# A written order of TensorE from the 21st attention tile on, and norm bounds of f64 weights from products of bf16 halves

## The chip, the cores and the metric

The kernel runs on one core of a Trainium2 chip. The metric is the device time of one execution in microseconds (us), the median of several runs. A core has five engines that run their own queues of instructions in order: PE (TensorE: matmuls, with their weight loads PEld), DVE (VectorE), ACT (ScalarE), POOL (GpSimd) and SP (SyncE, which here only issues DMAs). They wait for each other by semaphores. TensorE multiplies 128x128 weights (lhsT) with a moving operand (rhs) and adds into PSUM, which has eight banks per partition; the other engines work on SBUF and PSUM.

## The reference

Three blocks follow each other: attention with a threshold instead of a full softmax, a gated MLP with RMS norm whose weights come as f64, and a mixture of 8 experts whose gates are balanced by eight rounds of row and column normalisation.

```python
# q, k, v: 4 batches x 8 heads x 576 x 64
scores = scale * np.matmul(q, k.transpose(0, 1, 3, 2))
scores = np.where(scores >= np.max(scores, axis=-1, keepdims=True) - tau, scores, -1e9)
attn = np.exp(scores - np.max(scores, axis=-1, keepdims=True)); attn /= sum + 1e-9
x = attn @ v                                   # as 2304 x 512
xn = x / rms(x) * rms_g
x = silu(xn @ w_gate) * (xn @ w_val) @ w_out   # 512 -> 1536 -> 512, w_* in f64
P = balanced(exp(x @ w_gate2))                 # 2304 x 8
out = sum over e of P[:, e:e+1] * (relu(x @ w1[e]) @ w2[e])   # 512 -> 1024 -> 512
```

## The kernel before

**Precision.** Every f32 operand is written as a sum of two f16 words, high and low, after a scale by a power of two, and a product is three matmuls: high by high, high by low, low by high (`passes`). The scale of a weight comes from a bound on the norms of its columns.

**Attention.** The 36 rows of 128 or 64 queries (4 batches, 4 rows of 128 and one of 64) give 144 attention tiles: a tile is a row and a head (or two heads of the short row). `att_tile` makes S with four matmuls of 128x288 (L303), its row maximum on VectorE (L317), exp on ScalarE (L321), the threshold mask on VectorE (L323), and the two f16 words hl of e on ScalarE (L328) and GpSimd (L329, L330). `turn` transposes hl into eT by a DMA that SP issues. Four tiles later (LAG) `att_values` multiplies eT with v, 14 matmuls or 28 in the short rows (pv, L360). S has two PSUM tiles, pv one. When the 8 tiles of a row are done, `end_main` or `end_rem` divides by the sums and `finish_x` norms the row and transposes it into xnT.

**MLP.** Two rows together are a group j of 256 tokens. `mlp_in(j)` makes for each of 12 blocks f of the hidden width one PSUM tile gv (two halves, gate and value, 12 matmuls of 128x256 each, L557), from which ScalarE's tanh and two VectorE instructions make u (L565 to L567) and ScalarE and GpSimd the two words tT (L571, L572). `mlp_out(j)` makes two PSUM tiles x2 of 36 matmuls of 128x512 (L591), scales them and sends them to memory, transposed later as xo. gv and x2 share two PSUM tiles, tag mm. Groups 0 to 6 run during attention, 7 and 8 behind it.

**The weights of the MLP.** They come as f64. `words` loads a block of 128x512 of them as pairs of 32-bit words; `to_f32` rebuilds f32 from them: a Prelu on ScalarE that rescales the high word (L462), a shift of the low word on VectorE (L463), and an or of both on VectorE (L465). `prep_in` does so for a third of w_gate or w_val (four blocks kk). To bound the norms, ScalarE squares each block in bf16 (L483), and a matmul of 128x512 with the squared g of the RMS norm (gsq, L484) sums the squares of each column over partitions and blocks; VectorE takes the maximum over the 512 columns (L486), and all partitions hold it, since the weight operand is broadcast. Then come the scale, and the two f16 words (L492, L493). `prep_out` does the same for w_out, with squares and their row sums on ScalarE (L517, a Square whose accumulator is read) and a maximum over all partitions by `all_max`: a matmul with the identity and a reduction over 128 columns (L134, L136). `stage` is memory of wo in which three thirds of weights can be converted at a time; psx is one PSUM tile (tag mx) for all of these sums.

**What orders the work.** The code is handed to a scheduler that gives each engine its queue by priorities: attention stands ahead of the MLP (`attention_order`), and within that the scheduler takes what it holds to be ready; so gv, S and pv come in an order that the code doesn't spell out. `issue_after` only ties pv of an old tile behind S of a new one. `prepare` loads and converts q, k and v of the next batch in between. Behind attention a written order of TensorE already exists for the experts. There the weights of the first expert are loaded into w1r and w2r as soon as the memory of attention is free (L785), their maxima taken on VectorE (L790), and w1mxp is the matmul of that maximum.

## Time and profile before

| | us |
|---|---|
| median of 3 runs | 2075.53 (2074.88 to 2076.74) |
| profiled execution | 2072.64 |
| its span | 2070.8 |
| busy: PE | 1937.3 |
| busy: DVE | 1622.1 |
| busy: POOL | 1351.4 |
| busy: ACT | 1297.6 |

The span goes from the first to the last instruction of the profiled execution; the time of that execution is 1.84 us longer. Busy times are shares of the whole span, over stages that differ: the front with the weights' conversion up to about 143 us, attention with the MLP up to 601.6 us, the last groups of the MLP up to 728 us, and the experts. A time within the span is counted from its start.

### The profile page before, as it was taken

How to read it: one execution, taken by the hardware profiler on the slowest of the kernel's cores; microseconds unless marked ns; L12 is line 12 of the kernel's file. 1: busy time of each engine (PE TensorE's matmuls, PEld its weight loads, DVE VectorE, ACT ScalarE, POOL GpSimd, SP SyncE). 2: the span in 40 equal slices, each digit the busy share in tenths (PEclk: the TensorE clock that was granted, in tenths of full speed). 3: DMA queues.
4: the chain of work that ended last, by engine and by line, in shares of the span. 5: the costliest groups of instructions: out<-in, count | busy, mean ns of one | idle time of the engine just before them, and what ended most of it. 6: DMA issues, size and time to landing. Idle time of an engine off the chain costs nothing.

```text
span 2070.8 us, 43792 instructions
## 1 busy us (share of the span) xinstructions
PE 1937.3 (94%) x16462; PEld 1445.0 (70%) x16462; DVE 1622.1 (78%) x3364; ACT 1297.6 (63%) x2804; POOL 1351.4 (65%) x1412
## 2 busy tenths in 40 slices
PE   1558899899999998999999999999999999999998
PEld 0246676777777766777777777777777777777777
DVE  6998777778754546998888888888887888888865
ACT  6998778878753365657555555555555555555542
POOL 0457664666654476777677777776777777777754
PEclk9569999999999999999999999999999999999999
DMA  9987878977748665334434433444443434334332
GB/s 296 261 177 128 163 160 147 184 129 139 129 83 213 144 158 169 110 118 143 128 120 134 131 116 119 130 131 127 128 139 122 122 117 143 120 120 128 105 97 82
DMA packets 373093, 290.46 MB, mean 140 GB/s; under 512 B 286160, under 2 KB 299344, under 8 KB 372880
## 3 DMA queue, kind: packets, MB, share of 16 engines
q1 hardware_dynamic: 371712, 285.81, 53.6%
q8 instruction: 129, 2.11, 0.4%
q0 software_dynamic: 640, 1.84, 0.3%
q14 instruction: 84, 0.69, 0.1%
q10 hardware_dynamic: 528, 0.02, 0.0%
HBM read 195.71 MB, written 21.23 MB: 105 GB/s over the span
## 4 chain that ended last, share of the span: by engine, by line
PE 65%; DVE 3%; POOL 1%; DMA 1%; issue 1%; ACT 1%; SPq 0%; DVEq 0%; POOLq 0%; ACTq 0%
PE P L1127 30%; PE X L1059 17%; PE Z L1059 13%; PE gv L557 3%; PE x L591 2%; DVE w L766 1%; DMA xo<-x2d 1%; DVE acc L1141 0%; SPq L871 0%; DVE h L1038 0%; PE logits L913 0%; DVE lg L1005 0%; POOL w2s L833 0%; DVE w1m L790 0%; POOL h L1038 0%
## 5 line engine op out<-in xcount | busy, mean ns | idle before, releaser
L1127 PE MATMUL P<-w,h 128*128 128x256 f16 x6048 | 769.9, 273 | 2.7 <-DVE acc L1141 1.8
L1127 PEld LDWEIGHTS <-h 128*128 128x128 f16 x6048 | 591.4, 98 | 145.7 <-issue 9.8
L1059 PEld LDWEIGHTS <-w 128*128 128x128 f16 x4032 | 394.6, 98 | 195.6 <-issue 4.6
L1137 DVE SCALAR_TENSOR_TENSOR acc<-P,coef,acc 128x256 f32<-128x256 f32 x882 | 409.7, 477 | 81.7 <-PE P L1127 73.0
L1059 PE MATMUL X<-xo,w 128*128 128x384 f16 x2304 | 437.7, 327 | 1.3 <-ACT u2b L1079 0.9
L1059 PE MATMUL Z<-xo,w 128*128 128x384 f16 x1728 | 327.7, 326 | 1.5 <-DMA xo<-x2d 1.5
L329 POOL TENSOR_TENSOR hl<-e,hl 128x512 f16<-128x512 f32 x144 | 172.9, 1201 | 193.7 <-ACT hl L328 135.6
L557 PE MATMUL gv<-xnT,wg 128*128 128x256 f16 x1296 | 162.9, 274 | 14.7 <-DVE u L567 13.4
L557 PE MATMUL gv<-xnT,wv 128*128 128x256 f16 x1296 | 165.0, 273 | 0.0
L557 PEld LDWEIGHTS <-wg 128*128 128x128 f16 x1296 | 124.7, 98 | 33.7 <-issue 16.0
L591 PE MATMUL x<-wo,tT 128*128 128x512 f16 x648 | 144.2, 379 | 0.0
L323 DVE SCALAR_TENSOR_TENSOR e<-S,nt,e 128x576 f32<-128x576 f32 x144 | 116.5, 811 | 28.5 <-ACT e L321 28.0
L557 PEld LDWEIGHTS <-wv 128*128 128x128 f16 x1296 | 125.5, 98 | 14.7
L317 DVE TENSOR_REDUCE nt<-S 128x1 f32<-128x576 f32 x144 | 106.7, 750 | 25.1 <-PE S L303 22.8
L360 PE MATMUL pv<-vs,eT 128*128 128x64 f16 (+1 forms) x2240 | 97.1, 200 | 30.9 <-DMA eT<-hl 30.8
L360 PEld LDWEIGHTS <-eT 128*128 128x128 f16 (+1 forms) x2240 | 87.3, 105 | 52.9 <-DMA eT<-hl 40.3
L572 POOL TENSOR_TENSOR tT<-u,tT 128x256 f16<-128x256 f32 x108 | 74.9, 695 | 69.7 <-ACT tT L571 69.6
L321 ACT ACTIVATE e<-S,nt,c 128x576 f32<-128x576 f32 x144 | 117.4, 818 | 0.0
L591 PEld LDWEIGHTS <-tT 128*128 128x128 f16 x648 | 62.1, 98 | 70.7
L328 ACT ACTIVATE hl<-e 128x576 f16<-128x576 f32 x144 | 96.8, 677 | 21.3 <-DMA eT<-hl 10.4
L303 PE MATMUL S<-kT,qT 128*128 128x288 f16 (+1 forms) x320 | 65.2, 310 | 26.3 <-DVE e L323 19.7
L766 DVE SCALAR_TENSOR_TENSOR w<-w1r,w_s,w 128x512 f16<-128x512 f32 x64 | 84.1, 1328 | 7.1 <-ACT w L765 7.0
(2536 smaller groups left out, 3623.2 us busy)
## 6 DMA issues: line engine op xcount, KB each, us to landing
xo<-x2s SPq DMA_DIRECT2D x319, 384.0 KB, 3.1
w1r<-in_moe_w_dram SPq DMA_DIRECT2D x17, 1024.0 KB, 5.0
w2r<-in_moe_w_dram SPq DMA_DIRECT2D x17, 1024.0 KB, 6.1
x2s<-xo SPq DMA_DIRECT2D x17, 384.0 KB, 2.8
wgatew<-in_moe_w_gate_dram SPq DMA_DIRECT2D x12, 512.0 KB, 5.6
wo<-in_moe_w_out_dram SPq DMA_DIRECT2D x12, 512.0 KB, 4.6
wvalw<-in_moe_w_val_dram SPq DMA_DIRECT2D x12, 512.0 KB, 5.1
qX<-qT SPq DMA_DIRECT2D x40, 128.0 KB, 2.7
```

The lines of the kernel that those rows point to most:

```text
L317: V.tensor_reduce(mx, sv, AX.XY, ALU.max)
L321: A.activation(ev, sv, AF.Exp, bias=nt[:, 0:1], scale=st["c2"][:, c : c + 1])
L323: V.scalar_tensor_tensor(ev, sv, nt[:, 1:2], ev, ALU.is_ge, ALU.mult, accum_out=sums[:, slot : slot + 1])
L328: A.activation(hl[:, 0:S], e, AF.Copy)
L329: G.tensor_tensor(hl[:, S + REM :], e[:, 0 : NCH * P], hl[:, 0 : NCH * P], ALU.subtract)
L360: T.matmul(o, lhsT=a, rhs=r, start=n == 0, stop=n == len(mm) - 1)
L557: T.matmul(gv[:, a, :], lhsT=w[:, l, kk, f * P : (f + 1) * P], rhs=xt[:, r * KD + kk, :], start=n == 0, stop=n == 3 * KD - 1,)
L591: T.matmul(ps, lhsT=tT[f][:, l, o : o + P], rhs=wo[:, f, r, :], start=n == 0, stop=n == 3 * KF - 1,)
L766: V.scalar_tensor_tensor(dst[1], src, s, dst[0], ALU.mult, ALU.subtract)
L1059: T.matmul(ps, lhsT=w[:, a, l, kk, f * P : (f + 1) * P], rhs=xb[:, r * 2 + kk, :], start=n == 0 and j in (0, 1, 3), stop=n == 5, skip_grou ...
L1127: T.matmul(ps, lhsT=hs[u, ao, f][:, l, jj * P : (jj + 1) * P], rhs=w2[h][:, bo, r, f, :], start=n == 0 and j in (0, 1, 3), stop=n == 5, sk ...
L1137: main[True] = V.scalar_tensor_tensor(y, ps, coef[h][:, i : i + 1], y, ALU.mult, ALU.add)
```

## The change

Two things change.

First, the norms. The columns' sums of squares are no longer made. For each block `gram` multiplies the upper halves of its f32 words, read as bf16 with a step of two, with themselves, in four products of 128x128; all of a third of the weight add into one PSUM tile of 128x128, whose largest entry bounds the norm. VectorE reduces 128 columns instead of 512, and `all_max` takes the maximum over the partitions. g enters as its own maximum, a scale by a power of two (`gn`, `i_g0`, `ig2`). w_out's bounds come the same way, in three groups of four blocks. In `prep_in` the low word is no longer shifted on VectorE: ScalarE copies the 16-bit half that holds its upper bits, scaled and shifted down, into an integer. In `prep_out` the shift stays on VectorE and the Squares go.

Second, the order. From the end of the second row of queries on, TensorE's queue is the order of the code. The MLP becomes a generator: each attention tile now calls `mlp_step`, which gives one gv tile (24 matmuls) or a third of an x2 tile (12 matmuls). A group's steps start WAIT = 3 tiles behind its second row. `prep_out` stands ahead of group 0, with a priority offset of −300.

```diff
-    waiting, spot = [], [0]
+    waiting, spot, ordered = [], [0], []
     LAG = 4
+    WAIT = 3
...
         if len(waiting) == LAG:
-            with tc.issue_after(last.ins):
+            with ExitStack() as es:
+                if not ordered:
+                    es.enter_context(tc.issue_after(last.ins))
                 att_values(*waiting.pop(0))
...
+    gm = small([P, 1], "gmax")
+    V.tensor_reduce(gm, g_sb, AX.X, ALU.max, apply_absolute_value=True)
+    s_g, i_g0 = pow2_scale(all_max(gm, "gmx0", True), 1, 0, "rms")
+    gn = small([P, KD], "gn")
+    V.tensor_scalar(gn, g_sb, s_g[:, 0:1], None, ALU.mult)
+    ig2 = small([P, 1], "ig2")
+    V.tensor_tensor(ig2, i_g0, i_g0, ALU.mult)
+
+    def gram(ps, raw, first, last):
+
+        w = raw.bitcast(BF16).rearrange("p (n t) -> p n t", t=2)
+        for c in range(DM // P):
+            blk = w[:, c * P : (c + 1) * P, 1]
+            T.matmul(
+                ps, lhsT=blk, rhs=blk, start=first and c == 0, stop=last and c == DM // P - 1
+            )
+
+    def gram_bank(name):
+
+        return psx.tile([P, P], F32, tag="mx", name=name, bufs=1)
...
-    def to_f32(dst, word, name):
+    def to_f32(dst, word, name, engine=None):
...
-        V.tensor_scalar(lw, word[:, :, 0], 29, None, ALU.logical_shift_right)
+        if engine is A:
+            half = word.bitcast(U16).rearrange("p n (w t) -> p (n w) t", t=4)
+            A.activation(lw, half[:, :, 1], AF.Copy, scale=2.0**-13, bias=2.0**-15 - 0.5)
+        else:
+            V.tensor_scalar(lw, word[:, :, 0], 29, None, ALU.logical_shift_right)
         di = dst.bitcast(I32)
         V.scalar_tensor_tensor(di, di, 3, lw, ALU.logical_shift_left, ALU.bitwise_or)
-        return lw
...
-        ps = psx.tile([P, DM], F32, tag="mx", name=f"{name}n{gi}", bufs=1)
+        ps = gram_bank(f"{name}n{gi}")
...
-            to_f32(raw[:, kk], wd, f"{name}l{gi}_{kk}")
-            sq = pw.tile([P, 2 * P], F32, tag="u", name=f"{name}q{gi}_{kk}", bufs=2).bitcast(BF16)
-            A.activation(sq, raw[:, kk], AF.Square)
-            T.matmul(ps, lhsT=gsq[:, kk : kk + 1].to_broadcast([P, P]), rhs=sq, start=kk == 0, stop=kk == KD - 1)
-        n2 = small([P, 1], name + "n2", bufs=2)
+            to_f32(raw[:, kk], wd, f"{name}l{gi}_{kk}", A)
+            gram(ps, raw[:, kk], kk == 0, kk == KD - 1)
+        n2 = small([P, 1], "wn2", bufs=2)
         V.tensor_reduce(n2, ps, AX.X, ALU.max)
-        s, inv = norm_scale(n2, 1, 9, f"{name}{gi}")
-        gs = small([P, KD], f"{name}gs{gi}")
-        V.tensor_scalar(gs, g_sb, s[:, 0:1], None, ALU.mult)
+        s, inv = norm_scale(all_max(n2, "wnx"), 1, 9, f"{name}{gi}")
+        gs = small([P, KD], "wgs", bufs=3)
+        V.tensor_scalar(gs, gn, s[:, 0:1], None, ALU.mult)
...
-        V.tensor_scalar(a, i_g, 1.0 / 32.0, None, ALU.mult)
+        V.tensor_scalar(a, i_g, i_g0[:, 0:1], 1.0 / 32.0, ALU.mult, ALU.mult)
         g32.append(a)
-        V.tensor_tensor(igv[:, gi : gi + 1], i_g, i_v, ALU.mult)
+        V.scalar_tensor_tensor(igv[:, gi : gi + 1], i_g, ig2[:, 0:1], i_v, ALU.mult, ALU.mult)
...
-        om = small([P, KF], "om")
+        om = small([P, NG], "om")
         for f in range(KF):
             wd = words(bits[f * P : (f + 1) * P, :], f"wo{f}", ("x2", "x2t")[f % 2])
-            sq = to_f32(wo32[:, f], wd, f"wol{f}").bitcast(BF16)[:, 0:DM]
-            A.activation(sq, wo32[:, f], AF.Square, accum_out=om[:, f : f + 1])
+            to_f32(wo32[:, f], wd, f"wol{f}")
+            if f % n == 0:
+                ps = gram_bank(f"wog{f}")
+            gram(ps, wo32[:, f], f % n == 0, f % n == n - 1)
+            if f % n == n - 1:
+                V.tensor_reduce(om[:, f // n : f // n + 1], ps, AX.X, ALU.max)
         for _ in range(2):
-            V.tensor_tensor(
-                om.rearrange("p (g f) -> p g f", g=NG),
-                om.rearrange("p (g f) -> p g f", g=NG),
-                igv.to_broadcast([P, NG, n]),
-                ALU.mult,
-            )
+            V.tensor_tensor(om, om, igv, ALU.mult)
...
-    def mlp_in(j, hook=None):
+    def in_steps(j, tT, hook=None):
         xt = xnT.pop(j)
-        tT = []
...
+            yield
+
+    def mlp_in(j, hook=None):
+        tT = []
+        for _ in in_steps(j, tT, hook):
+            pass
...
+    def mlp_steps(j):
+        tT = []
+        yield from in_steps(j, tT)
+        yield from out_steps(j, tT)
+
+    def out_steps(j, tT, pool=None):
...
+                if n % KF == KF - 1 and n < 3 * KF - 1:
+                    yield
...
+            if a == 0:
+                yield
...
-            if o == o0 + 2:
+            if o == o0 + 4:
...
+    steps = []
+
+    def mlp_step(t):
+
+        while steps and steps[0][0] <= t:
+            if next(steps[0][1], 0) is None:
+                return
+            steps.pop(0)
...
+    with ExitStack() as order:
+        for t in range(len(row) + LAG):
...
+                for g in done:
+                    (end_main if g["c"] < NCH else end_rem)(g)
+                mlp_step(t)
...
-            i = g["i"]
...
-                    tc.tile_pool(name="psm", bufs=2, space=PSUM, side="right")
-                )
-                for gi in range(NG):
-                    prep_group(gi)
-                first = tc.cur_priority
-                tT = mlp_in(0)
-                prep_out()
-                mlp_out(0, tT)
-            elif i is not None and i % 2 == 1 and i < len(tiles) - 3:
-                mlp_out(i // 2, mlp_in(i // 2))
+                i = g["i"]
+                if i == 1:
+                    pse_cm.__exit__(None, None, None)
+                    psm = ctx.enter_context(
+                        tc.tile_pool(name="psm", bufs=2, space=PSUM, side="right")
+                    )
+                    for gi in range(NG):
+                        prep_group(gi)
+                    first = tc.cur_priority
+                    with tc.high_priority(offset=-300):
+                        prep_out()
+                    order.enter_context(tc.manual_schedule(engines={mybir.EngineType.PE}))
+                    ordered.append(True)
+                if i is not None and i % 2 == 1 and i < len(tiles) - 3:
+                    steps.append((t + WAIT, mlp_steps(i // 2)))
+        while steps:
+            mlp_step(t + WAIT)
     psa_cm.__exit__(None, None, None)
     pa_cm.__exit__(None, None, None)
```

On TensorE around the first gv tile, before (a name reads tile_batch_row_head for S, tile_group_block for gv, and the first matmul of each run of one tile is shown):

```order
L360 MATMUL pv0_2_1860<-vs0_0_229,eT0_2_3_1875 128x64
...
L557 MATMUL gv0_0_1228<-xnT0_595,wg_102 128x256
...
L557 MATMUL gv0_1_1260<-xnT0_595,wg_102 128x256
...
L303 MATMUL S0_3_0_2013<-kT0_0_171,qT0_3_794 128x288
...
L360 MATMUL pv0_2_1860<-vs0_1_232,eT0_2_4_1915 128x64
...
L303 MATMUL S0_3_1_2048<-kT0_0_171,qT0_3_794 128x288
...
L360 MATMUL pv0_2_1860<-vs0_1_232,eT0_2_5_1950 128x64
...
L557 MATMUL gv0_2_1291<-xnT0_595,wg_102 128x256
```

and in the changed kernel:

```order
L458 MATMUL wog4_1340<-wo_102 128x128
...
L579 MATMUL gv0_0_1585<-xnT0_610,wg_100 128x256
...
L303 MATMUL S0_2_7_1617<-kT0_1_205,qT0_2_526 128x288
...
L362 MATMUL pv0_2_1480<-vs0_0_244,eT0_2_3_1495 128x64
...
L579 MATMUL gv0_1_1651<-xnT0_610,wg_100 128x256
...
L303 MATMUL S0_3_0_1683<-kT0_0_186,qT0_3_809 128x288
...
L362 MATMUL pv0_2_1480<-vs0_1_247,eT0_2_4_1535 128x64
...
L579 MATMUL gv0_2_1718<-xnT0_610,wg_100 128x256
```

Before, gv0_0 and gv0_1 stand together and then two pairs of S and pv; in the changed kernel each gv tile of 24 matmuls is followed by the S and pv of one attention tile. wog4 are the products of w_out's halves.

On TensorE at the end of attention, before (pv3_4 are the last values of batch 3; the last line of them here is the last tile's, 28 matmuls):

```order
L360 MATMUL pv3_4_9764<-vs3_0_8033,eT3_4_0_9662 64x64
...
L557 MATMUL gv6_5_8578<-xnT6_7929,wg_102 128x256
...
L360 MATMUL pv3_4_9764<-vs3_1_8128,eT3_4_6_9793 64x64
...
L557 MATMUL gv6_6_8609<-xnT6_7929,wv_103 128x256
...
L557 MATMUL gv6_11_8765<-xnT6_7929,wg_102 128x256
...
L591 MATMUL x2_12_8796<-wo_104,tT6_0_8450 128x512
...
L591 MATMUL x2_13_8842<-wo_104,tT6_0_8450 128x512
...
L557 MATMUL gv7_0_9932<-xnT7_9189,wg_102 128x256
```

and in the changed kernel:

```order
L628 MATMUL x2_12_9565<-wo_102,tT6_4_9062 128x512
...
L628 MATMUL x2_12_9565<-wo_102,tT6_8_9324 128x512
...
L628 MATMUL x2_13_9716<-wo_102,tT6_0_8791 128x512
...
L303 MATMUL S3_4_6_9777<-kT3_1_7392,qT3_4_9227 64x288
...
L362 MATMUL pv3_4_9871<-vs3_0_7612,eT3_4_0_9703 64x64
...
L579 MATMUL gv7_1_10072<-xnT7_8841,wg_100 128x256
...
L362 MATMUL pv3_4_9871<-vs3_1_7811,eT3_4_6_9900 64x64
...
L579 MATMUL gv7_3_10138<-xnT7_8841,wg_100 128x256
```

What was behind the last pv (gv6_6 to gv6_11, x2_12, x2_13) stands ahead of it now; gv7_0 does too.

On VectorE behind attention, before:

```order
L567 SCALAR_TENSOR_TENSOR u7_0_9957<-u7_0_9957,gv7_0_9932 128x256
L566 SCALAR_TENSOR_TENSOR u7_1_9989<-u7_1_9989,gv7_1_9964 128x256
L567 SCALAR_TENSOR_TENSOR u7_1_9989<-u7_1_9989,gv7_1_9964 128x256
L790 TENSOR_REDUCE w1m_9926<-w1r1_9928 128x1
L566 SCALAR_TENSOR_TENSOR u7_2_10021<-u7_2_10021,gv7_2_9996 128x256
L567 SCALAR_TENSOR_TENSOR u7_2_10021<-u7_2_10021,gv7_2_9996 128x256
L790 TENSOR_REDUCE w1m_9926<-w1r1_9928 128x1
L566 SCALAR_TENSOR_TENSOR u7_3_10055<-u7_3_10055,gv7_3_10030 128x256
L567 SCALAR_TENSOR_TENSOR u7_3_10055<-u7_3_10055,gv7_3_10030 128x256
L790 TENSOR_REDUCE w2m_9927<-w2r1_9930 128x1
```

and in the changed kernel:

```order
L588 SCALAR_TENSOR_TENSOR u7_5_10230<-u7_5_10230,gv7_5_10205 128x256
L589 SCALAR_TENSOR_TENSOR u7_5_10230<-u7_5_10230,gv7_5_10205 128x256
L588 SCALAR_TENSOR_TENSOR u7_6_10261<-u7_6_10261,gv7_6_10236 128x256
L589 SCALAR_TENSOR_TENSOR u7_6_10261<-u7_6_10261,gv7_6_10236 128x256
L845 TENSOR_REDUCE w1m_10034<-w1r1_10036 128x1 x2
L588 SCALAR_TENSOR_TENSOR u7_7_10292<-u7_7_10292,gv7_7_10267 128x256
L845 TENSOR_REDUCE w2m_10035<-w2r1_10038 128x1 x2
L589 SCALAR_TENSOR_TENSOR u7_7_10292<-u7_7_10292,gv7_7_10267 128x256
L588 SCALAR_TENSOR_TENSOR u7_8_10324<-u7_8_10324,gv7_8_10299 128x256
L589 SCALAR_TENSOR_TENSOR u7_8_10324<-u7_8_10324,gv7_8_10299 128x256
```

The maxima of the first expert weights, w1m and w2m, stood behind u7_1 to u7_4, one at a time; now two stand behind u7_6 and two inside u7_7.

## Rows read from the trace of the kernel before

**Rows 1.** The page: busy time of each engine; the chain that ended last, by engine.

```profile
PE 1937.3 (94%) x16462; PEld 1445.0 (70%) x16462; DVE 1622.1 (78%) x3364; ACT 1297.6 (63%) x2804; POOL 1351.4 (65%) x1412
...
PE 65%; DVE 3%; POOL 1%; DMA 1%; issue 1%; ACT 1%; SPq 0%; DVEq 0%; POOLq 0%; ACTq 0%
```

**Rows 2.** Windows: stretch, length, busy time (instructions) of engines, clock, DMA share, GB/s.

```profile
0.00:143.30 143.30, 54.15 (x395) 29.30 (x396) 120.04 (x286) 118.79 (x247) 43.29 (x53) 0.70 0.98 255
143.30:200.00 56.70, 48.79 (x554) 39.93 (x552) 48.92 (x123) 52.00 (x127) 44.35 (x54) 1.00 0.64 116
200.00:601.60 401.60, 381.13 (x4288) 290.01 (x4286) 306.35 (x709) 313.60 (x725) 252.20 (x346) 1.00 0.80 149
601.60:728.20 126.60, 125.98 (x943) 91.63 (x941) 59.08 (x131) 44.95 (x92) 52.28 (x67) 1.00 0.63 150
```

**Rows 3.** Windows, the same columns: the front.

```profile
40.00:143.30 103.30, 50.13 (x387) 28.52 (x387) 99.70 (x221) 92.38 (x197) 41.11 (x45) 0.59 0.99 241
```

**Rows 4.** Timeline of TensorE: start, duration, what, out<-in, tile, count.

```profile
196.08 3.83 PE L591 MATMUL x<-wo,tT 128*128 128x512 f16 x17
...
600.85 0.97 PE L360 MATMUL pv<-vs,eT 128*64 128x64 f16 x28
...
602.96 1.47 PE L557 MATMUL gv<-xnT,wg 128*128 128x256 f16 x12
604.27 1.47 PE L557 MATMUL gv<-xnT,wv 128*128 128x256 f16 x12
...
616.06 15.70 PE L591 MATMUL x<-wo,tT 128*128 128x512 f16 x72
```

**Rows 5.** Groups of VectorE, 0 to 145 us: count | busy, mean ns | idle before.

```profile
L463 DVE TENSOR_SCALAR wvall<-wvalw 128x512 int32<-128x512 int32 x12 | 5.2, 437 | 0.0
L463 DVE TENSOR_SCALAR wgatel<-wgatew 128x512 int32<-128x512 int32 x12 | 4.9, 420 | 3.6 <-DMA wgatew<-in_moe_w_gate_dram 3.6
L486 DVE TENSOR_REDUCE wgaten<-wgaten 128x1 f32<-128x512 f32 x3 | 2.0, 680 | 0.0
```

**Rows 6.** Timeline of VectorE: the maximum of wo's norms over the partitions.

```profile
138.05 0.17 DVE L526 TENSOR_REDUCE om<-om 128x1 f32<-128x12 f32 x1
...
138.80 0.28 DVE L136 TENSOR_REDUCE womx<-womxp 128x1 f32<-128x128 f32 x1
```

**Rows 7.** Groups of ScalarE, 0 to 145 us.

```profile
L462 ACT ACTIVATE wo<-wgatew 128x512 f32<-128x512 f32 x12 | 7.5, 650 | 0.0
L517 ACT ACTIVATE wol<-wo 128x512 bf16<-128x512 f32 x12 | 7.5, 624 | 2.9 <-DVE wo L465 2.9
L483 ACT ACTIVATE wgateq<-wo 128x512 bf16<-128x512 f32 x12 | 7.2, 623 | 0.0
...
L517 ACT ACTIVATION_READ_ACCUMULATOR wol<-wo 128x1 f32 x12 | 2.3, 194 | 0.0
```

**Rows 8.** Groups of TensorE, 0 to 145 us: the products with g squared.

```profile
L484 PE MATMUL wgaten<-wgateq,gsq 128*128 128x512 bf16 x12 | 6.8, 598 | 12.9 <-ACT wgateq L483 12.9
```

**Rows 9.** Waits of TensorE, 150 to 600 us: total us, times, longest us.

```profile
PE gv L557 <- DVE u L567: 12.7, 13, 2.6
PE pv L360 <- DMA eT<-hl: 12.1, 15, 1.6
```

**Rows 10.** Timeline of VectorE at the end of attention.

```profile
601.86 0.86 DVE L425 TENSOR_TENSOR xrem<-pv,rsumr 64x256 f32<-64x256 f32 x2 [0.88 <-PE pv L360]
...
622.04 0.75 DVE L383 SCALAR_TENSOR_TENSOR xn<-xrem,rs,xn 128x512 f16<-128x512 f32 x1 [0.85 <-ACT xn L382]
...
638.54 1.21 DVE L790 TENSOR_REDUCE w1m<-w1r 128x1 f32<-128x1024 f32 x1
```

**Rows 11.** Timeline of SP, which issues DMAs, at the end of attention.

```profile
624.11 0.57 SPq L785 DMA_DIRECT2D w1r<-in_moe_w_dram  x1
...
625.30 12.26 SPq L871 DMA_TRANSPOSE xo<-x2d  x7
```

**Rows 12.** The loads of tile w1r, 600 to 680 us.

```profile
DMA to landing us min/median/max: 5.8/5.9/6.0
```

53 lines of the change are left out of this document (24 added, 29 removed).

## The prediction

> **What bounds the kernel now.** I first read the busy line and the chain that ended last: TensorE is busy 94% of the span, and the chain runs over TensorE for 65% of it with nothing else above 3% [rows 1]. So the span is TensorE's work plus TensorE's idle time, and a change can only win by removing idle time or matmuls. Next I read the stretches, to see where the idle time lies [rows 2]. Span less TensorE's busy time is 89.15 us up to 143.3 us (before the first gv), 7.9 us from there to 200, 20.5 us from 200 to the end of attention at 601.6, 0.6 us from there to 728.2. The rest of the span, the last stage, has 2070.8 − 1937.3 − 118.2 = 15.3 us; its order is the same in both kernels, so I carry it over unchanged. The change can therefore act on three places: the front, the 20.5 us, and the seam at 601.6 us, which now costs nothing.
>
> In the front TensorE is not the bound. Between 40 and 143.3 us VectorE is busy 99.70 of 103.30 us and ScalarE 92.38, TensorE 50.13 at a mean granted clock of 0.59 [rows 3]. VectorE is full, ScalarE has a tenth to spare, and the DMA share is 0.99, which is a third candidate. ScalarE stays as full up to 200 us (52.00 of 56.70, [rows 2]): wo's low and high words and the next batch's norms are still in its queue while gv0 runs. So the front ends at about x2_0, which starts at 196.08 us [rows 4], and I price its parts by how much earlier that instruction can start.
>
> **Part one, norm bounds and low words.** On VectorE 24 shifts go, 12 at 0.437 and 12 at 0.420 us, 10.3 us [rows 5]. The six 512-wide reductions (0.68 each, 4.1 us in all) become two 128-wide ones each, 0.28 us by the one reduction of that form shown, wo's maximum [rows 6], 3.4 us: 0.7 us less. VectorE saves 11 us. On ScalarE the 24 Squares (0.622 us) become 24 Copies that read a 16-bit half of each word. No row shows that form. The nearest is the Prelu of the same step, which also reads a strided word and takes 0.650 us, so I bound a Copy by 0.62 and 0.71 and take 0.65: between nothing and 2.1 us more, 0.7 us taken. The 12 Squares of wo with their readouts go: 0.624 + 0.194 us each by the rows, 9.8 us, but consecutive ScalarE instructions overlap by some 0.1 us, so I count 0.52 + 0.1 us, 7.4 us [rows 7]. ScalarE saves 6.7 us (5.3 to 9.8). On TensorE 24 matmuls of 512 columns become 144 of 128 columns, 18432 columns against 12288; it is idle over half of that stretch, and I cost them at nothing. If that cover were gone, 6144 more columns at the 0.598 us per 512 of the old product [rows 8] would be 7.2 us.
>
> The new bounds also need a maximum over the partitions: reduction, small matmul, reduction, 0.86 us from the end of the one to the end of the other in the one place that does so today (wo's, 138.22 to 139.08 us, [rows 6]). Six of them are 5.2 us of latency, hidden while another weight's words are converted (there are three stages), and otherwise exposed.
>
> Both engines must shrink for the front to shrink. VectorE falls by 11 us and ScalarE by 6.7, so I take 7 us at x2_0. Low end 2 us, if the maxima are exposed or the loads bound it (share 0.99); high end 11 us, VectorE's whole saving. That prep_out stands before gv0 only changes the order within this sum; 16 products of wo and the maximum, some 2 us of TensorE at these rates, now stand between gv0_2 and gv0_3 and are in it.
>
> Here the Trainium skill speaks against the change: "ScalarE: Activation LUTs", section "Rules for kernel authors", says that adds and multiplies belong on VectorE and not on ScalarE. By this rule the shifts would stay on VectorE, whose saving would be 0.7 us instead of 11; x2_0 would come 0.7 us earlier and the sum below would be −0.7 − 7 + 3.3 = −4.4, 2071 us instead of 2065. The rows say that one shift is indeed shorter on VectorE (0.43 against about 0.65 us), and that VectorE is nonetheless the fuller engine; I go by the rows.
>
> **Part two, the written order.** Before, gv tiles come two or three in a row, S in pairs and pv in runs of 28; after, each attention tile carries one piece of MLP: 24 gv matmuls (2.62 us: two twelves that start 1.31 us apart) or 12 of x2 (15.70 us for 72, so 2.62 us) [rows 4]. With the S and pv of a tile, some 0.9 us, that is 3.5 us. Of the idle time in this stretch gv waits 12.7 us on u (13 times), pv 12.1 us on the transposed e (15 times) [rows 9]. The first kind is a burst outrunning the two gv banks, and goes when gv and attention alternate. The second is the DMA behind a burst of S, and should halve. But a written order can't fill a wait with other work, so those that stay are paid in full. VectorE is busy 306 and ScalarE 314 of the 401.6 us [rows 2], 76 and 78%, so on average there is room. I take 20.5 us down to 13.5, a gain of 7. Bounds: a gain of 17, all but 3.5 us gone, and a loss of 15.
>
> **Part three, the end of attention.** Today the last pv ends at 601.8 us, and behind it stand gv6_6 to gv6_11 and x2_12, x2_13, 30 us of TensorE [rows 4]. Under these run the chain that the first expert weights wait for: xrem at 601.86, xn17 done at 622.79, its transposes on SP, w1r issued at 624.11, its maxima on VectorE from 638.54 [rows 10, 11]. After, gv6 and nearly all of x2_12 and x2_13 stand ahead of the last pv. The chain's own work from the last pv to w1r's issue is about 6.6 us by my estimate (xrem 0.9, two ScalarE passes of the length of those above, three short steps and xn's 0.75, about 4, and a transpose's issue, 12.26 us for 7, so 1.75), and its landing 5.9 us more [rows 10 to 12], so the maxima can start 12.5 us behind the last pv. But VectorE has them between u7_6 and u7_7, which TensorE reaches at 11 and 13.5 us. Two reductions of 1.21 us, and two of w2r1 between u7_7's halves, hold back u7_7 until 17.9 us; gv7_9, which needs its bank, wanted it at 15.9: 2.0 us. w1r0, behind five transposes on SP, lands at about 21 us, and u7_9 stands behind its two reductions, so gv7_11 loses about 1.3 us. Together 3.3 us; none if the loads come sooner, 8 us if the transposes of e and x2 crowd SP. Nothing later is late: the order from gv8_0 on is the same.
>
> **Sum.** −7 − 7 + 3.3 = −10.7 us. The profiled execution took 2072.64 us, 1.84 above its span; less 10.7 that is 2061.9. The median of the three runs, 2075.53, lies 2.9 above the profiled one; so I predict 2065 us.
>
> **Rivals.** *Neutral.* The front is bound by its loads (share 0.98 to 0.99, [rows 2, 3]) and gains 2 us; the order swaps gv's waits for pv's and gains 2; the seam takes 3.3: −0.7, about 2075 us. For it: the loads' share, and TensorE at 94%. Against: VectorE, not the DMA, is what has no idle time.
> *Slower.* The written order stalls TensorE in every gv tile: u, exp, e and hl of one tile must all be done inside 3.5 us, and a pv whose transpose is behind a raw load stops everything, since nothing may pass it. Half a microsecond in each of the 84 gv tiles of this stretch (seven groups of 12) is 42 us in place of 20.5: −7 + 21.5 + 3.3 = +17.8, 2093; at 0.35 us each it is 29.4, +5.2, and 2081 us. It decides from 28.4 us of idle time between x2_0 and the last pv on, where the sum reaches +4.2. Against: 76 and 78% busy engines, and four tiles of lag between S and its pv, some 14 us.
> *Dense.* Front and order both reach their upper ends, 11 and 17 us, less 3.3: −24.7, 2051 us. For it: gv's waits are all of one cause.
> *It does not do what it says*: if TensorE's bound products wait in the front for halves that ScalarE and VectorE finish no sooner, nothing moves ahead of x2_0 and the order alone is left, −7 + 3.3, 2072 us; I count it with the neutral one.
>
> **How the numbers follow.** Forecast (2058 to 2071) 0.55, dense 0.13, neutral 0.16, slower 0.16. A measurement of this kernel can tell about 0.2%, 4.2 us: faster is below 2071.4, slower above 2079.7. Forecast and dense with a little of the neutral case give faster 0.69; the rest of the neutral case is 0.15; slower 0.16. The range leaves out the worst of the slower case and the best of the dense one: 2054 to 2079.
>
> **What would show it.** Front: x2_0 at about 189 us instead of 196.1, VectorE still full to 130 us, the new Copy at 0.62 to 0.71 us. Order: the last pv ends at about 588 us; idle time of TensorE between x2_0 and there about 13.5 us, gv's wait on u nearly gone. Seam: gv7_9 and gv7_11 wait some 3 us on u. I am wrong if x2_0 doesn't move by at least 2 us, if pv's waits on the transposed e grow, or if w1r's maxima come so late that the stall at the seam is above 8 us.

## The result: slower by 0.56%, and the profile after

| | before | after |
|---|---|---|
| median, us | 2075.9 (2073.7 to 2078.1, 6 runs) | 2086.9 (2082.0 to 2090.4, 6 runs) |
| ratio | | 1.0056, 95% interval 1.0043 to 1.0069 |
| profiled execution | 2072.64, span 2070.8 | 2082.69, span 2080.9 |
| busy PE / DVE / ACT | 1937.3 / 1622.1 / 1297.6 | 1947.8 / 1607.8 / 1297.6 |

The forecast, 2065 us in a range of 2054 to 2079, was wrong in its sign. The profiled execution of after lies 4.2 us below the median of its runs, so where this text works with profiles it accounts for some 10 us. The profiled executions below lie within about 4 us of the median of their kernel's runs, those of e12_seam and e11_order_xn 5 and 7 us from it.

The page of after (busy times and shares, then the shares of the chain that ended last; these answer to [rows 1]):

```profile
PE 1947.8 (94%) x16589; PEld 1458.8 (70%) x16589; DVE 1607.8 (77%) x3357; ACT 1297.6 (62%) x2780; POOL 1345.2 (65%) x1412
PE 70%; DVE 4%; POOL 1%; DMA 1%; ACT 1%; SPq 1%; issue 1%; DVEq 0%; POOLq 0%; ACTq 0%
```

VectorE has 14 us less to do, and the span is 10.1 us longer. TensorE's idle time over the span, 2080.9 − 1947.8 = 133.1 us, is that of before (133.5): what was won in the front was lost behind it, and the rest of the span's growth reads as busy time. Busy is not work: the same matmul counts twice as long at the lower level of the clock. So I split every stage. I matched the trace's matmuls one by one with the kernel's order (the profile leaves tile numbers out), took the starts of some first matmuls as marks (these marks lie 0.2 us ahead of the times on the timelines), and split each length into work (a matmul of gv 0.109 us, of x2 0.216, of S 0.122, of pv 0.030, as they take at 2.4 GHz), idle time, and the loss to the clock (busy time times one less the granted clock, added up over short slices). What is left over is 0 to 4 us a stage.

| stage (start of its last mark) | before | after |
|---|---|---|
| to gv0_0 | 143.3 | 138.9 |
| gv0_0 to x2_0 | 52.5: idle 7.9, clock 0 | 59.1: idle 9.5, clock 5.1 |
| x2_0 to gv1_0 | 23.3: idle 1.5, clock 0 | 30.4: idle 7.4, clock 0 |
| gv1_0 to gv7_3 | 420.1: idle 19.0, clock 1.6 | 418.3: idle 16.3, clock 6.2 |
| gv7_3 to the first expert's X | 39.2: idle 0, clock 0 | 43.5: idle 2.4, clock 1.7 |
| from there to the end | 1392.3 | 1390.6 |

Between gv0_0 and the first X the matmuls' work is the same (500 and 501 us). Idle time grows by 7.2 us, the loss to the clock by 11.4. The clock, for which the prediction had no term, is the larger half.

The stretches of after (columns: busy time and instructions of PE, PEld, DVE, ACT, POOL, granted clock, DMA share, GB/s), which answer to [rows 2, 3]:

```profile
0.00:138.90 138.90, 56.23 (x495) 36.81 (x495) 108.23 (x259) 111.44 (x224) 40.23 (x54) 0.78 1.07 253
138.90:198.00 59.10, 49.62 (x535) 41.21 (x535) 49.11 (x124) 47.30 (x111) 38.65 (x45) 0.91 0.48 109
198.00:646.60 448.60, 424.64 (x4599) 321.31 (x4600) 315.41 (x755) 336.02 (x762) 266.23 (x367) 0.98 0.70 138
```

The last pv ends at 646.6 us (601.6 before): as planned, groups 0 to 6 now stand ahead of it nearly whole.

**A stop and what it costs twice.** TensorE's longest stop of after, on its timeline (start, duration, engine, line, operation; in brackets the idle time before it and who ended it) and in slices of 4 us:

```profile
218.73 2.76 PE L628 MATMUL x<-wo,tT 128*128 128x512 f16 x12
228.67 2.72 PE L579 MATMUL gv<-xnT,wg 128*128 128x256 f16 x12 [7.18 <-ACT x2f L650]
...
224.00:228.00 4.00, 0.00 (x0) 0.00 (x0) 3.77 (x11) 2.98 (x9) 0.00 (x0) 0.61 0.94 200
228.00:232.00 4.00, 3.33 (x18) 2.40 (x19) 0.00 (x0) 1.25 (x3) 3.74 (x6) 0.54 0.90 270
232.00:236.00 4.00, 4.00 (x49) 3.59 (x47) 1.50 (x3) 2.24 (x5) 1.62 (x3) 1.00 0.99 253
```

TensorE did nothing for 7.18 us; then twelve matmuls of gv took 2.72 us instead of 1.47, at a granted clock of 0.54, the 1.2 GHz level. Such stretches follow the stops that end at 156.5 us (3.89 us long), 179.1 (2.77), 228.7 (7.18), 299.3 (3.18), 369.0 (3.89) and 664.8 (1.97). Before, there is one after the front, at 526 to 529 us. Not every stop has one behind it: in e11_order_xn, a kernel further below, the matmuls of gv behind a stop of 3.46 us go on at a granted clock of 1.00 and take 1.47 us as ever, and so they do behind one of 3.03 us at 371.8 us.

```profile
225.76 1.47 PE L560 MATMUL gv<-xnT,wg 128*128 128x256 f16 x12 [3.46 <-DVE u L570]
227.07 1.47 PE L560 MATMUL gv<-xnT,wv 128*128 128x256 f16 x12
```

The profile names ScalarE's x2f as what ended the stop before 228.67. It ended then, at 228.62, but that matmul also reads xnT, and SP's timeline shows where xnT was:

```profile
212.12 0.40 SPq L156 DMA_DIRECT2D raw_k<-in_k_dram  x1
212.57 1.36 SPq L161 DMA_DIRECT2D raw_k<-in_k_dram  x2
214.09 4.04 SPq L342 DMA_TRANSPOSE eT<-hl  x1
...
225.28 1.34 SPq L389 DMA_TRANSPOSE xnT<-xn  x1
```

The row xn was normed at 207.9 us. Its transpose was issued at 225.28, behind raw_k of batch 2 and five transposes of keys, queries and e, of which the one behind raw_k took 4.04 us to issue; it lands 3.3 us later, at 228.5.

### The profile page after: what moved, and what is told of

Read it like the earlier page. It is cut to its first block, busy times and chain, and to the rows that moved or that the text cites. A ratio compares the mean times of both kernels' runs of the same rounds, so it can differ in the third digit from the quotient of the medians.

```text
span 2080.9 us, 43956 instructions
## 1 busy us (share of the span) xinstructions
PE 1947.8 (94%) x16589; PEld 1458.8 (70%) x16589; DVE 1607.8 (77%) x3357; ACT 1297.6 (62%) x2780; POOL 1345.2 (65%) x1412
## 4 chain that ended last, share of the span: by engine, by line
PE 70%; DVE 4%; POOL 1%; DMA 1%; ACT 1%; SPq 1%; issue 1%; DVEq 0%; POOLq 0%; ACTq 0%
PE P L1182 30%; PE X L1114 17%; PE Z L1114 13%; PE gv L579 5%; PE x L628 3%; PE S L303 1%; PE pv L362 1%; SPq L926 1%; DVE w L821 1%; DMA xo<-x2d 1%; DVE acc L1196 0%; DVE w1m L845 0%; DVE h L1093 0%; DMA w1r<-in_moe_w_dram 0%; DVE e L325 0%
## 5 line engine op out<-in xcount | busy, mean ns | idle before, releaser
L331 POOL TENSOR_TENSOR hl<-e,hl 128x512 f16<-128x512 f32 x144 | 169.1, 1175 | 211.0 <-ACT hl L330 143.5
L628 PE MATMUL x<-wo,tT 128*128 128x512 f16 x648 | 150.3, 382 | 2.6 <-DVE u L589 2.6
L330 ACT ACTIVATE hl<-e 128x576 f16<-128x576 f32 x144 | 97.6, 678 | 44.0 <-DVE e L325 41.9
```

Of the source, the lines that this page charges most:

```text
L330: A.activation(hl[:, 0:S], e, AF.Copy)
L331: G.tensor_tensor(hl[:, S + REM :], e[:, 0 : NCH * P], hl[:, 0 : NCH * P], ALU.subtract)
L628: T.matmul(ps, lhsT=tT[f][:, l, o : o + P], rhs=wo[:, f, r, :], start=n == 0, stop=n == 3 * KF - 1,)
```

## Experiments: the two parts apart

Theory one: the front gained, and the written order lost more than that. Theory two: the front's change itself costs, and the order is nearly neutral.

**e1_order**, the written order with the old norms (a diff here is against the changed kernel where nothing else is said):

```diff
-            to_f32(raw[:, kk], wd, f"{name}l{gi}_{kk}", A)
-            gram(ps, raw[:, kk], kk == 0, kk == KD - 1)
+            to_f32(raw[:, kk], wd, f"{name}l{gi}_{kk}")
+            sq = pw.tile([P, 2 * P], F32, tag="u", name=f"{name}q{gi}_{kk}", bufs=2).bitcast(BF16)
+            A.activation(sq, raw[:, kk], AF.Square)
+            T.matmul(ps, lhsT=gsq[:, kk : kk + 1].to_broadcast([P, P]), rhs=sq, start=kk == 0, stop=kk == KD - 1)
...
```

> The written order alone, with the old norms (Squares, products with g squared, low words shifted on VectorE). Theory one, the loss comes from the written order: TensorE stops where a gv tile's input or an S bank is late, each stop of 2 us or more is followed by a spell at the lower granted clock, and the last groups no longer cover the first expert loads. Then the order alone shows the same kind of stops and costs at least as much as the whole change did, +9 to +16 us: 2085 to 2092. Theory two, the loss comes from the new norms (bound products in the front at the lower clock, the 3.9 us stop for wo's maximum): then the order alone is within 4 us of the kernel before, 2072 to 2080.

Measured 2078.7 us, 1.0019 (1.0008 to 1.0030): 3 us slower.

**e2_norms**, the new norms in the scheduler's order:

```diff
-            if o == o0 + 4:
+            if o == o0 + 2:
...
-    with ExitStack() as order:
+    for t in range(len(row) + LAG):
```

> The new norm bounds and low words alone, TensorE's queue left to the scheduler as before and the scales of k and v two tiles earlier as before. Theory one (the order costs): the front's gain is kept, the first gv about 4 us earlier, and nothing is lost later: 2068 to 2074. Theory two (the norms cost): 2080 to 2088, with TensorE's busy time up by more than 4 us against the kernel before.

Measured 2085.2 us, 1.0050 (1.0031 to 1.0069): 9.6 us slower. The parts add, 3 + 10, to about the 11 of both. By the times theory two holds: the kernel with the part that I had taken to be the safest has most of the loss. Stage by stage (lengths in us):

| | before | after | e1_order | e2_norms | e4_xn |
|---|---|---|---|---|---|
| to gv0_0 | 143.3 | 138.9 | 143.6 | 135.3 | 138.9 |
| to x2_0 | 52.5 | 59.1 | 51.0 | 54.1 | 59.2 |
| to gv1_0 | 23.3 | 30.4 | 27.0 | 29.5 | 24.2 |
| to gv7_3 | 420.1 | 418.3 | 417.1 | 431.2 | 425.3 |
| to X | 39.2 | 43.5 | 47.3 | 39.2 | 46.2 |
| from gv0_0 to X: idle, clock | 28.4, 1.6 | 35.6, 13.0 | 31.3, 8.4 | 38.3, 9.7 | 34.0, 14.9 |

e2_norms has its first gv 8 us sooner, x2_0 6.4 sooner, which is what I had forecast, and gv1_0 no sooner (218.9 against 219.2). Nearly all that it loses to the kernel before it loses behind that mark, 431.2 us up to gv7_3 against 420.1. Whether that is the norms' doing is asked below (e10_before_nowof). In the written order e1_order and the changed kernel differ in the norms alone: 8 us by the medians, with intervals that don't overlap, and in the profiles the changed kernel is 4.7 us ahead at gv0_0 and 6.8 us behind at gv1_0.

## Experiments on the norms: why the front's gain is not kept

**e7_gram**, e2_norms with the low words shifted on VectorE as before:

```diff
-            to_f32(raw[:, kk], wd, f"{name}l{gi}_{kk}", A)
+            to_f32(raw[:, kk], wd, f"{name}l{gi}_{kk}")
```

> The new bounds alone, with the low words shifted on VectorE as before; TensorE's queue left to the scheduler. In the kernel with both parts of the norms (2085) the 24th Prelu of the gate and value weights came at 90.5 us instead of 80.3, and wo's last load at 145.0 instead of 128.9. Theory one: the copies on ScalarE hold the words' buffers and so the loads; then this one is back at 2070 to 2078, its 24th Prelu near 80 us. Theory two: the bounds' own chain does it (product, reduction, maximum over the partitions in one PSUM tile, per third of a weight): 2081 to 2088, with the late Prelus and loads unchanged.

Measured 2088.7 us, 1.0063 (1.0046 to 1.0080). The kernel is 3.5 us slower without the low words on ScalarE, but the intervals overlap and the scheduler's order scatters by more (below), so a gain from them isn't shown; the loss is there without them too. In the prediction I weighed a rule of the Trainium skill ("ScalarE: Activation LUTs", section "Rules for kernel authors": adds and multiplies belong on VectorE). The Copy costs more on ScalarE, 0.648 to 0.655 us against 0.43 on VectorE, as the rule has it, and the kernel is still no slower for it.

What is late is the weights. The 24th Prelu of w_gate and w_val starts at 94.7 us (80.5 before), the last one of wo at 148.3 (133.2; in e1_order 133.8, in e2_norms 150.2). The stretch before, then after:

```profile
60.00:100.00 40.00, 21.64 (x161) 12.03 (x159) 40.00 (x92) 35.33 (x72) 16.01 (x16) 0.54 1.04 256
100.00:140.00 40.00, 17.26 (x174) 11.36 (x175) 37.22 (x78) 35.77 (x84) 18.07 (x20) 0.54 0.93 200
...
60.00:100.00 40.00, 20.98 (x192) 13.28 (x191) 38.96 (x81) 37.84 (x77) 14.13 (x16) 0.64 1.12 256
100.00:140.00 40.00, 22.24 (x232) 16.35 (x233) 34.51 (x76) 30.45 (x61) 19.11 (x24) 0.59 1.05 212
```

From 100 to 140 us neither VectorE (34.5 of 40) nor ScalarE (30.5) is full any more; the DMA share is 1.05 where it was 0.93, and the bytes per second hardly grow. From 60 to 140 us the two engines' waits for words grow from 4.3 to 8.1 us. Yet wo's loads land hardly later behind their issue, 4.8 us against 4.6 (w_gate's 7.4 against 5.6); they are issued later, the last at 144.6 us (129.2 before). SP's queue of after, between the fifth load of wo and the next two:

```profile
105.56 6.87 SPq L342 DMA_TRANSPOSE eT<-hl  x3
112.47 3.07 SPq L277 DMA_TRANSPOSE qT<-qs  x1
115.70 1.32 SPq L342 DMA_TRANSPOSE eT<-hl  x1
...
120.19 1.36 SPq L389 DMA_TRANSPOSE xnT<-xn  x1
121.71 1.31 SPq L342 DMA_TRANSPOSE eT<-hl  x1
123.07 1.06 SPq L474 DMA_DIRECT2D wo<-in_moe_w_out_dram  x2
```

From 100 to 140 us SP spends 34.0 of 40 us on issuing, 30.1 of them on 16 transposes; before it was 22.7, with 19.0 on 13. Three explanations: one load stands in a bad place on SP's queue; SP's queue as a whole is too slow; or the DMA engines are full whatever the order, and the slow issues are their doing.

**e13_pool**, the changed kernel with the words loaded from GpSimd's queue, and **e15_pool_before**, the same in the kernel before:

```diff
-        nc.sync.dma_start(out=r, in_=src)
+        G.dma_start(out=r, in_=src)
```

> The changed kernel, but the f64 weights' words are loaded by DMAs that GpSimd issues and not SP; nothing else is edited. Theory one, the loads of the weights stand on SP's queue behind the transposes of attention: they come sooner, the last load of w_gate and w_val by 75 us or earlier (83.7 in the changed kernel) and wo's loads end by 130 us (144.3), the first gv starts by 135 us, x2_0 by 190, and the time is 2076 to 2082 us instead of 2087. Rival, the DMA engines themselves are full (their share is above 1 in that stretch): the loads only change places with the transposes, the last loads move by less than 3 us, attention's own transposes get later, and the time stays at 2084 to 2090 or grows, as GpSimd's own work in front of each load holds it up.

> The kernel before with the f64 words loaded from GpSimd's queue. If SP's queue held the loads of this kernel as well (its DMA share was 0.99 in that stretch): the first gv by 138 us or earlier (143.3), and 2069 to 2073 us. If VectorE, which has no idle time there, is what bounds this front, as the prediction said: gv0_0 within 2 us of 143.3 and 2073 to 2079 us.

Measured 2107.1 us, 1.0144 (1.0126 to 1.0162), and 2092.9 us, 1.0082 (1.0063 to 1.0102). wo's last Prelu comes at 147.6 us, no sooner than in the changed kernel, and with the old norms at 145.5, 12 us later than in the kernel before; gv0_0 starts at 162.2 and 156.7. The transposes of e and of keys up to 170 us (operation, count, median us from issue to landing), of before, after and e13_pool in turn:

```profile
eT<-hl SPq DMA_TRANSPOSE x26, 3.5
kT<-ks SPq DMA_TRANSPOSE x15, 3.4
...
eT<-hl SPq DMA_TRANSPOSE x27, 4.6
kT<-ks SPq DMA_TRANSPOSE x15, 3.8
...
eT<-hl SPq DMA_TRANSPOSE x23, 4.9
kT<-ks SPq DMA_TRANSPOSE x10, 5.4
```

The transpose of e takes a third longer after the change, and both take longer again when loads run beside them from a second queue. That speaks for the rival of these runs, that the DMA engines are full. The Trainium skill ("DMA: Bandwidth & Descriptors", section "Issuing engines are not separate DMA queues") says that DMAs of every issuing engine interleave on the same 16 engines, and that a second one saves only the time of issuing. Here it saved nothing and cost 20 us. But the runs don't show full engines to be the cause: GpSimd has the loads in one queue with its own work for attention (between its last four loads of wo stand eight of its steps on hl, L331 and L332), and no run separates a slow issuing queue from full DMA engines.

**f1_rawv** and **f3_rawv_norms** put one load back. In the changed kernel, batch 1's raw_v (1 MB) stands ahead of the last five words of w_gate and w_val on SP; a tie holds it behind them, as it stood before:

```diff
-        nc.sync.dma_start(out=r, in_=src)
+        d = nc.sync.dma_start(out=r, in_=src)
+        if tag == "tT":
+            word_load[:] = [d]
...
-            nx["raw_v"] = load_raw("v", v, b + 1)
+            with ExitStack() as es:
+                if not early:
+                    es.enter_context(tc.issue_after(word_load[0].ins))
+                nx["raw_v"] = load_raw("v", v, b + 1)
```

> The changed kernel, with one tie more: batch 1's raw_v is loaded behind the last words of w_gate and w_val on SP, as it stood in the kernel before; in the changed kernel it stood ahead of the last five of them. Theory one, that place of a 1 MB load, and the transpose of e that took 6.52 us behind it, made the weights late: the last Prelu of w_val starts by 85 us (94.7 in the changed kernel, 80.5 before), wo's last load is issued by 133 (140.0), wo's maximum by 145 (156.3), x2_0 by 192 (198.0), and the time is 2079 to 2083 us instead of 2087. Rival, the DMA engines are full whatever stands first: wo's last load and x2_0 stay within 3 us of those places, raw_v's norms get late instead, and the time is 2084 to 2090 us.

> The new norm bounds alone in the scheduler's order (2085.2 us), with batch 1's raw_v loaded behind the weights' words. Theory one, the place of that load cost the norms their gain: wo's last load is issued by 133 us, wo's maximum is taken by 148 (167.3), gv1_0 starts by 214 (218.9), and the time falls below 2080. Rival, the full DMA engines and the order that the scheduler deals anew keep it at 2082 to 2090 us.

Measured 2093.4 us, 1.0090 (1.0077 to 1.0103), 6 us slower than the changed kernel, and 2084.2 us, 1.0043 (1.0028 to 1.0058), not to be told from e2_norms. wo's last Prelu does come sooner, at 141.8 in f1_rawv (148.3) and 141.9 in f3_rawv_norms (150.2). But the first gv comes later, at 144.8 (138.9) and 145.4 (135.3), and in f1_rawv womxp stands at 157.4, where it stood. What the tie gives to wo it takes from the attention and the first gv: with a DMA share of 1.11 from 60 to 100 us and 1.12 to 140, the order chose who was late. As the explanation of the loss, the place of raw_v falls.

**e9_norms_nowof** and **e10_before_nowof** ask what the late wo costs. Its last step, twelve scalings into two words, is replaced by zeros, in e2_norms and in the kernel before:

```diff
-        rr = pw.tile([P, 4, HD], F32, tag="x2", name="wof")
...
-            V.tensor_scalar(r, wo32[:, f], sf[:, f // n : f // n + 1], None, ALU.mult)
-            A.activation(wo[:, f, 0, :], r, AF.Copy)
-            G.tensor_tensor(wo[:, f, 1, :], r, wo[:, f, 0, :], ALU.subtract)
+            G.memset(wo[:, f], 0.0)
```

> The new norms alone (queue left to the scheduler), with the last step of wo left out: its scaling on VectorE, its high word on ScalarE and its low word on GpSimd become 12 fills with zero on GpSimd, which wait for no scale. To be read against the kernel before with the same step left out. Theory one: the front's gain is lost because wo is ready 34 us later (its last scaling at 202.6 us instead of 168.8) and collides with the preparation of batch 1; then this kernel is at least as fast as its counterpart, by 0 to 8 us. Theory two: the loss is elsewhere: it stays 6 to 11 us slower than its counterpart.

> The kernel before with the last step of wo left out in the same way (12 fills with zero on GpSimd in place of scaling, high word and low word). Both theories: 2 to 8 us faster than the kernel before, 2068 to 2074, since VectorE and ScalarE are nearly full up to 200 us.

Measured 2069.9 us, 0.9974 (0.9961 to 0.9987), and 2079.0 us, 1.0019 (1.0009 to 1.0028). Without that step the new norms are 9 us faster than the old, where with it they are 10 slower. That looks as if the front's gain were there and wo's last step, which falls at 174 to 203 us in e2_norms and before at up to 171, used it up. The stages say otherwise. Without the step gv1_0 comes 3.5 us sooner with the new norms and 3.4 with the old, and e9 and e10 reach it 0.4 us apart; their 9 us arise behind it. e10 is also 3 us slower than the kernel before, with work left out: an edit of the front makes the scheduler deal attention anew. The stage from gv1_0 to gv3_0 has nearly the same work in it (130.5 us before, 131.8 to 133.6 in the others):

| scheduler's order | before | e2_norms | e7_gram | e9 | e10 | e15 | f3 |
|---|---|---|---|---|---|---|---|
| start of gv1_0, us | 219.2 | 218.9 | 223.7 | 215.4 | 215.8 | 233.9 | 224.2 |
| gv1_0 to gv3_0, us | 140.6 | 148.0 | 155.2 | 144.3 | 148.0 | 145.5 | 146.2 |
| gv1_0 to gv7_3, us | 420.1 | 431.2 | 431.1 | 422.4 | 430.1 | 426.1 | 429.7 |

All six edited orders are 4 to 15 us slower up to gv3_0 than the one before, 1 to 3 us of it by more work, and 2 to 11 us slower up to gv7_3. e10 and e15, which have the old norms, lose 10 and 6 us there, e2_norms 11. So the loss of e2_norms can't be told from this scatter. That the norms cost is shown best in the written order (e1_order against the changed kernel), although there too the scheduler still deals the queues of the other engines; what they are worth in the scheduler's order stays open, and so does what uses up the 6.4 us between x2_0 and gv1_0.

## Experiments on the order

**e4_xn**, the changed kernel with the end of a row (norm and transpose of xn) 200 places earlier in the priorities, against the stop at gv1_0:

```diff
-                for g in done:
-                    (end_main if g["c"] < NCH else end_rem)(g)
+                with tc.high_priority(offset=200):
+                    for g in done:
+                        (end_main if g["c"] < NCH else end_rem)(g)
```

> The changed kernel with the end of each row (its division, norm and transposes) 200 steps of priority earlier; on SP the second transpose of xnT1 now stands ahead of the load of k for batch 2, eight places earlier. Theory one: the stop of 7.2 us in front of gv1_0 is the landing of that transpose, and goes together with the spell of lower clock behind it: 6 to 9 us less than the changed kernel, 2078 to 2081. Rival: the stop is the release of the PSUM bank by ScalarE's x2f, as the profile names it, which stays where it is: no change at gv1_0, within 2 us.

Measured 2080.4 us, 1.0019 (1.0009 to 1.0029): 6.6 us less than after. SP's timeline of e4_xn:

```profile
210.49 1.31 SPq L389 DMA_TRANSPOSE xnT<-xn  x1
211.96 0.47 SPq L156 DMA_DIRECT2D raw_k<-in_k_dram  x1
212.48 1.37 SPq L161 DMA_DIRECT2D raw_k<-in_k_dram  x2
214.01 5.48 SPq L342 DMA_TRANSPOSE eT<-hl  x1
```

The transpose now stands ahead of raw_k, 15 us sooner; TensorE's idle time from x2_0 to gv1_0 goes from 7.4 us to nothing. In the profile most of it comes back one tile later:

```profile
231.11 2.72 PE L579 MATMUL gv<-xnT,wg 128*128 128x256 f16 x12 [4.61 <-DVE u L589]
```

The slow issue behind the 1 MB load stays: the next transpose takes 5.48 us to issue, and now it is one that nobody waits for so urgently. The profiled execution, 2083.3 us, is the slowest of nine, so where the gain of the median lies isn't shown.

**e11_order_xn**, the same edit on e1_order:

> The written order alone (old norms), with the end of each row 200 steps of priority earlier. In the order alone gv waits 9.0 us for the transposed rows xnT, four times, the largest single cause. Theory one: as in the changed kernel (2087 to 2080) these waits shrink and with them the spells of lower clock: 3 to 8 us less than the order alone, 2071 to 2076. Rival: the waits move to the next input that is late, within 2 us of 2078.7.

Measured 2079.8 us, 1.0022 (1.0009 to 1.0036), no better than e1_order, though the stage up to gv1_0 fell from 27.0 to 23.3 us in the profile and the seam by 3. Its runs spread from 2073 to 2087; the rival that I had put down holds by the median.

**e3_wait6**, the changed kernel with each group's MLP begun later:

```diff
-    WAIT = 3
+    WAIT = 6
```

> The changed kernel with a group's steps starting 6 tiles behind its second row instead of 3. Theory one: the stops in front of gv0_0 (2.8 us) and gv2_0 (3.2 us, its xnT lands 3.2 us late) go, with the spell of lower clock behind the second (2 us), and the three steps that now stand behind the last pv take some of the stop at the seam (2.0 us and its spell): 5 to 9 us less than the changed kernel, 2078 to 2082. Rival: the stops only move, since VectorE and ScalarE set the pace there: within 2 us of the changed kernel.

Measured 2086.0 us, 1.0053 (1.0037 to 1.0069), one less than after. The later stages did get shorter (gv1_0 to gv7_3 413.3 us, the seam 41.9), but gv0_0 starts at 154.6, 15.7 us later, and that takes all of it. As one number for all groups, WAIT gives at one end what it takes at the other.

**e12_seam**, e11_order_xn with one step of group 6's MLP on every second tile, so that 26 us of matmuls stand behind the last pv again:

```diff
+        if len(steps) == 1 and steps[0][2] == 6 and t < len(row) + LAG and t % 2:
+            return
         while steps and steps[0][0] <= t:
...
```

> The written order with the old norms and the earlier end of a row (the kernel of the last such run, 2079.8 us), but group 6 gives one step of MLP on every second attention tile, so that gv6_11, x2_12, x2_13 and gv7_0 to gv7_2, some 26 us of TensorE, stand behind the last pv again as they did in the kernel before. Theory one, the seam was paid because no matmuls were left behind the last pv to run under the chain to the first expert weights: from gv7_3's place in the stream the seam falls from 44.5 to 39 to 41 us, and as the attention in front has fewer matmuls per tile it loses 0 to 3 us there; 2074 to 2078 us. Rival, the time moves with it: the attention tiles of the last 20 become bound by VectorE and the transposes, TensorE idles there by as much as the seam gains or more, and the time is 2079 to 2084.

Measured 2085.3 us, 1.0042 (1.0027 to 1.0056). The seam is mended: 39.2 us, no idle time, as in the kernel before. But the attention ahead of it, which lost its filling, pays 17 us in its profile (gv5_0 to gv7_3 157.3 us against 140.5). By the medians the two kernels differ by 5.5 us only; the profiles are the slowest of the one and the fastest of the other. What TensorE waited for in that stretch, e11_order_xn and then e12_seam (us, times, longest):

```profile
PE gv L560 <- ACT x2f L631: 2.2, 1, 2.2
...
PE pv L364 <- DMA eT<-hl: 4.8, 4, 2.1
PE gv L560 <- ACT x2f L631: 3.5, 1, 3.5
PE pv L364 <- DVE x L410: 3.0, 3, 1.3
PE S L305 <- DVE e L327: 1.4, 2, 1.2
```

Waits of pv and S come back as soon as there is no gv between them. In these runs the matmuls of group 6 covered either the tiles of attention or its end, not both.

**f2_rawv_xn** and **e14_all** put mends together, e4_xn with f1_rawv's tie, and e4_xn with e12_seam's rule and e13_pool's loads:

> The changed kernel with both ties: batch 1's raw_v behind the weights' words, and the earlier end of a row that took 6.6 us off it (2080.4). Theory one: 2073 to 2077 us, even with the kernel before or under it. Rival: 2079 to 2082, no better than the earlier end of a row alone.

> The changed kernel with three mends together: the earlier end of a row, which took 6.6 us off it, group 6's MLP on every second tile, and the weights' words loaded from GpSimd's queue. By the sum of the theories (the stop at gv1_0, the seam and the late wo): 2080.4 less 3 for the seam less 5 for the loads, 2070 to 2075 us, below the kernel before. By the rivals (seam moved only, DMA engines full): 2079 to 2086.

Measured 2090.1 us, 1.0064 (1.0052 to 1.0076), and 2107.0 us, 1.0149 (1.0136 to 1.0163). e14_all comes out where e13_pool does, so the loads seem to decide it. f2_rawv_xn shows e4_xn's edit once more: 3.3 us less than f1_rawv, its idle time up to gv1_0 4.5 us instead of 13.7. No kernel that computes everything beat the one before.

## Why the prediction failed, step by step

- **Part one, −7 us at x2_0.** The prices were right for VectorE, with 14 us less to do, and for the Copy, 0.65 us. ScalarE's busy time did not fall by the 6.7 us of the sum: it is 1297.6 us in both, though its instructions' lengths add up to 9.7 less. The norms alone bring x2_0 6.4 us forward, near the 7, but the changed kernel has it 2.2 us later. The step that failed is the reading of [rows 3], that VectorE is full and so the front is VectorE's. The DMA share of 0.99 stood beside it, and I put it into the neutral rival with 0.16. After the change both engines have room from 100 us on, the loads are issued later, and wo's words are converted 15 us later instead of sooner. Whether the DMA engines or SP's queue hold the loads stays open.
- **"The front ends at x2_0."** It doesn't. In e2_norms 6.4 us at x2_0 are 0.3 at gv1_0: the stage between them, which I had taken to be carried along, grows from 23.3 to 29.5 us, and in the changed kernel to 30.4.
- **The new bounds' TensorE work at nothing.** Wrong for wo's maximum: a matmul in a written queue, it stopped everything behind it for 3.9 us (below), and a slow stretch of the clock followed. I had named that place and priced it at 2 us of work; in a written order it is a wait. e1_order, with the old norms in the same order, has no such stop behind its first gv; no run takes this one away alone.
- **Part two, −7 us.** By the measure of the forecast, idle time from x2_0 to the last pv, 20.5 us became 24.0 (448.60 − 424.64, in the stretches of after) and not 13.5. (The last pv could not end at 588 us, as I wrote, since by part three 30 us of matmuls now stand ahead of it.) The two waits that I named did shrink. From the waits of TensorE in 139 to 620 us of after, against 12.7 and 12.1 us in [rows 9]:

```profile
PE gv L579 <- ACT x2f L650: 9.2, 3, 7.2
PE S L303 <- DVE e L325: 6.0, 4, 3.9
PE gv L579 <- DVE u L589: 4.6, 2, 2.8
PE womxp L133 <- DVE om L549: 3.9, 1, 3.9
PE gv L579 <- ACT hl L330: 3.2, 1, 3.2
...
PE pv L362 <- DMA eT<-hl: 1.6, 3, 0.6
```

  In their place stand few and long ones, at the changes of group and batch: the next group's xnT, the next batch's keys, wo's maximum. I had written that a written order can't fill a wait, and applied it to the many small waits; it decides at the rare long ones. From gv1_0 to gv7_3 the gain is 2.7 us of idle time, and 4.6 us of it are lost again to the clock.
- **Part three, the seam, +3.3 us.** Right in mechanism and, by some luck, nearly in size, +4.3: 2.4 idle and 1.7 clock, where I had 3.3 of idle time alone. VectorE's timeline of after:

```profile
659.43 2.35 DVE L845 TENSOR_REDUCE w1m<-w1r 128x1 f32<-128x1024 f32 x2 [0.32 <-DMA w1r<-in_moe_w_dram]
661.69 0.41 DVE L588 SCALAR_TENSOR_TENSOR u<-u,gv 128x256 f32<-128x256 f32 x1
662.12 2.35 DVE L845 TENSOR_REDUCE w2m<-w2r 128x1 f32<-128x1024 f32 x2
664.38 0.41 DVE L589 SCALAR_TENSOR_TENSOR u<-u,gv 128x256 f32<-128x256 f32 x1
```

  Two maxima of w1r, half of u, two of w2r, the other half: gv7_9 waits 1.97 us at 664.84, where I had worked out 2.0. The slow clock behind it adds 1.7; the second wait of 1.3 that I expected is 0.4.
- **No term for the clock.** [Rows 3] show a mean granted clock of 0.59 in a stretch where TensorE is half idle. I read it as a property of the front. It was a price as well: after loses 13.0 us to the clock, 1.9 of them in the front's last slow stretch at 139 to 143 us and the rest, just under 2 us each, behind six stops of 2 to 7 us. This term, put at nothing without a reason, is the largest part of what was lost behind gv0_0, 11.4 us against the kernel before. That a stop doesn't always bring it (e11_order_xn) makes it hard to forecast.
- **The rivals.** The neutral one had the loads in view, which did come late, and the wrong time, since late loads don't only cap the gain: they move work into the next stage. The slower one had the right sign, with stalls in every tile; they came in six places.

## What to carry to other kernels

When one engine is full and the DMA share beside it is near 1, expect that relieving the engine may leave the stage to the loads and the queue that issues them, and follow the last thing that the stage delivers into the next stage before counting a gain. A written order removes the many short waits and makes the few long ones absolute, so look first at the inputs that arrive once a group or a batch, and at the queue on which they stand. Weigh a stop of TensorE by its length and by the slow clock that may follow it, and measure each edit against the scheduler's own scatter, here 4 us and more in one stage: an edit that leaves work out showed it.
